# Attention start of a fused attention and mixture-of-experts kernel: another order for the first two heads

## The chip, the cores and the metric

The kernel runs on one core of a Trainium2 chip. The metric is the device time of one execution in microseconds (us), as the median of several runs. The five engines are TensorE (PE, with its weight loads as PEld), VectorE (DVE), ScalarE (ACT), GpSimd (POOL) and SyncE (SP). SP only issues DMAs; ACT and POOL can issue DMAs too. Each engine takes its own instructions strictly in the order in which they were recorded.

## The reference, cut to what matters

Sixteen heads (2 batches of 8) of attention over 768 positions with 64 dimensions, masked by a hash: six signs of a projection give each query and each key a bucket, and only equal buckets see each other.

```
q_bits = (np.einsum('bhsd,dk->bhsk', q, proj) > 0)      # the same for k
mask = q_bucket[:, :, :, None] == k_bucket[:, :, None, :]
scores = np.where(mask, scale * np.matmul(q, k.transpose(0, 1, 3, 2)), -1e9)
scores = scores - np.max(scores, axis=-1, keepdims=True)
attn = np.exp(scores); attn = attn / (np.sum(attn, axis=-1, keepdims=True) + 1e-09)
return np.matmul(attn, v)
```

The result goes through a mixture of experts (8 experts, one per token, 1536 tokens of 512) and a gated two-layer network (512 to 2048 and back).

## The kernel before, in words

The program is one long list, written in the order in which it is to run: no scheduler moves anything. The attention comes first and ends near 230 us; the experts follow until about 397 us, then the two-layer network.

The attention works head by head. A head has four tiles, X, Y, K1 and K2 (one of four sets, taken in turn), which hold q and k, scaled and split into a high and a low part (hi and lo, made on ACT and by a subtraction), and rows that carry the hash signs (the bits). `prep0` fills the tiles of heads 0 to 2, `prep` those of the later heads, where SP's DMAs place hi, lo and bits (`put_bits`). `bits` makes the signs: products with the projection on PE into the tiles psb, then two sign operations on DVE into tile b.

Before a head's scores are taken, each row's maximum must be known. `mx` (line 454 on) multiplies X and K2 into tiles psm, two products of 384 columns for each sixth of the head, and DVE takes the maxima (line 457); there are three psm buffers. After the sixth part, DVE forms `top` (line 460), and SP sends it into row 76 of X (line 461). `scores(k)` (lines 466 to 474) is step k of 96, six steps to a head: four products (pst, from Y and K1 and from X and K2), and two exponentials on ACT into a tile pf. `high` rounds pf to 16 bits (phi, on ACT or DVE), `low` takes the rest (plo, a subtraction on POOL), and `pv` multiplies both with the values (psv). There are four pf buffers, so an exponential also waits for plo of four steps before, and two pst buffers.

The values are scaled by a power of two. `vmax` takes maxima of the values on DVE, `vscale` turns them into one scale for four heads: a transposition on PE (psn), a maximum on DVE, a product (pso), and some ten small DVE operations, the result being sc. `vsplit(h)` writes the scaled values of a head in 16 bits on ACT and their rest by a SCALAR_TENSOR_TENSOR on DVE (lines 717 to 719); `vgate` makes the gate's columns of the same tile (vh), by products psg, a copy gv, transpositions and four small DVE operations. `heat` issues PE products on a tile of zeros that nothing reads.

The steps from `run(pre[0])` to `first = ...` (lines 756 to 789) are written out by hand. After that a loop over k issues in turn `scores(k)`, the roundings, `mx` of later parts as the table entry `ac` says, and `pv`; `at`, `spread` and `stages` place all other work at fractions of k, from the numbers in the table Q.

Of the kernel before, what the change touches and what calls it, by code (L numbers as in the profile page):

```python
# [13 lines left out]
AF = mybir.ActivationFunctionType  # L14
ALU = mybir.AluOpType
# [5 lines left out]
B, H, S, D = 2, 8, 768, 64  # L21
# [42 lines left out]
def moe_attention_kernel(ctx, tc, qk, v, vt, pj, wg, w1, w2, win, wout, out, cap):  # L64
# [8 lines left out]
    def f32(t):  # L73
        return t.bitcast(F32)

    def run(gen):
        for _ in gen:
            pass
# [229 lines left out]
                )  # L308


    Q = {'v': (-3.25, -4.75, -1.75, -2.25), 'vg': (-6.5, -6.75), 'vgd': 1, 'pr': (-13.0, -12.75, -12.0, -12.5), 'prd': 0.6, 'b0': 7.75, 'b': 1.75, 'bd': 0.5, 'vm0': (9.0, 9.25, 10.75, 13.0), 'vm': (-0.5, 4.75, 7.0, 12.25), 'vs': 13.25, 'pa': 1.5, 'ev': 0.5, 'lvt': -5.0, 'v4': (2.0, 4.25, 8.0, 16.25), 'vg0': (1.85, -4.4, 8.0), 'p2': 3.5, 'lr': (0.25, 1.25, 5.5), 'lv': 6.25, 'vsd': 0.75, 'ac': (0, 0, 2, 4, 6, 7, 8, 10), 'hd': (3, 5, 17), 'hn': (1, 3, 2, 0, 2, 0, 0, 0), 'ap': (0,), 'h0': (7,), 'hl': (6,), 'l0': (), 'll': (1, 3), 'ht': (6, 3, 7, 6, 3, 2)}


    HT = Q["ht"]
# [1 line left out]
    with ExitStack() as actx:  # L316
# [13 lines left out]
        def heat(pool_, tag, n, cols=512):  # L330

            if pool_ not in heat_t:
                heat_t[pool_] = pool_.tile([P, 512], F32, tag=tag, name=f"heat{tag}")
            for _ in range(n):
                pe.matmul(heat_t[pool_][:, :cols], idle_sb[:, 0:P], idle_sb[:, :cols], start=True, stop=True)  # L335
# [22 lines left out]
        def load_r(h):  # L358
            rt[h] = pr.tile([P, S], F32, tag="r", name=f"r{h}")
            sp.dma_start(out=rt[h], in_=qk[h])  # L360
# [47 lines left out]

        def put_bits(h):
            st = sets[h % 4]  # L410
            b = b_t[h // 4]
            o = 32 * (h % 4)
            sp.dma_start(out=f32(st["X"])[D : D + 12], in_=f32(b)[o : o + 12])
            sp.dma_start(out=f32(st["K2"])[D : D + 12], in_=f32(b)[o + 12 : o + 24])

        def signs(out, ps, c):
            dve.tensor_scalar(out=out, in0=ps, scalar1=0.0, scalar2=c, op0=ALU.is_gt, op1=ALU.subtract)
# [45 lines left out]
        def scores(k):  # L463
            h, j = divmod(k, NC)
            st = sets[h % 4]
            pf = pf_t[k] = pt.tile([P, S], F32, tag="pf", name=f"pf{k}", bufs=4)
            kc = slice(j * P, (j + 1) * P)
            for n in range(2):
                ps = ps_t.tile([P, 512], F32, tag="t", name=f"pst{k}{n}")
                qc = slice(n * HS, (n + 1) * HS)  # L470
                pe.matmul(ps[:, :HS], st["K1"][:, kc], st["Y"][:, qc], start=True, stop=False)  # L471
                pe.matmul(ps[:, :HS], st["K2"][0:77, kc], st["X"][0:77, qc], start=False, stop=True)  # L472
                act.activation(  # L473
                    pf.rearrange("k (c n p) -> k c n p", c=NC, n=2)[:, :, n],
                    ps[:, :HS].rearrange("k (p c) -> k c p", c=NC), AF.Exp, scale=0.125 / SC / SC,
                )
# [234 lines left out]
        def vsplit(h):  # L711
            g = h // 4
            r = vr_t[g][:, h % 4]
            s = sc_t[g][:, 0:1]
            t = vh(h)
            o = E * (1 - h % 2)
            act.activation(t[:, :, o : o + D], r, AF.Copy, scale=s)
            yield
            dve.scalar_tensor_tensor(
                out=t[:, :, VA + o : VA + o + D], in0=r, scalar=s, in1=t[:, :, o : o + D],  # L720
                op0=ALU.mult, op1=ALU.subtract,
            )
            dve.memset(t[:, :, DE:VA], 1.0)
            if h > 3:
                c = t[:, :, VA + o : VA + o + 1]
                pool.tensor_copy(c, c)
# [37 lines left out]
        b0 = bits(0, [ps_v.tile([P, 512], F32, tag="v", name=f"psb0{n}") for n in range(2)])  # L764
        for n in range(NC):
            mx(n)
        run(pre[1])
        load_r(4)
        next(b0)
        for i in range(4):  # L770
            vmax(0, i)
        vs = vscale(0)
        next(vs)
        next(vs)
        next(b0)
        heat(ps_t, "t", 2)
        next(vs)
        next(vs)
        next(b0)
        put_bits(1)  # L780
        scores(0)
        run(b0)
        run(vs)
        next(pre[2])
        put_bits(2)
        run(pre[2])
        first = vsplit(0), vgate(0)
        next(first[1])
        next(first[1])
# [20 lines left out]
        def at(k, f, *args):  # L810
            later.setdefault(k, []).append((f, args))

        def spread(k, gen, d=1):


            def part(k):
                if next(gen, gen) is not gen:
                    n = k + (d if k < STEPS - NC * 2 else min(d, 1) * 0.75)
                    at(n, part, n)

            at(k, part, k)

        def stages(gen, ks):
            for k in ks:
                at(k, next, gen, None)

        stages(first[1], (1, 1.5, 2, 2.75, 3.25))
        spread(1, first[0], 0.75)
        for i in range(3):
            at(Q["lr"][i], load_r, 5 + i)  # L830
        for g in range(1, G):
# [7 lines left out]
            at(max(0, 24 * (h // 4 - 1) - 2) + h % 4 / 4, load_r, h)  # L839
        for h in range(3, NH):  # L840
            if h == 3:
                spread(2.25, prep(h), 3)
            else:
                spread(NC * h + Q["pr"][h % 4], prep(h), Q["prd"])
        for h in range(1, NH):
# [711 lines left out]
```

## Time and profile before

| | |
|---|---|
| Median of 3 runs | 661.85 us (661.36 to 662.96) |
| Profiled execution | 664.08 us |
| Its span | 662.3 us |
| PE busy | 630.1 us (95%) |
| PEld busy | 469.5 us (71%) |
| DVE busy | 472.1 us (71%) |
| ACT busy | 435.1 us (66%) |
| POOL busy | 232.2 us (35%) |
| Chain that ended last | PE 55%, ACT 3%, DMA 3%, DVE 2% |

Busy shares are means over stages with different limits. The change lies in the first 60 us, so only rows of that stretch tell what it moves, and rows of the later stages tell whether a shift of the start reaches the end. PE's busy time counts a product from its start to its modelled end, and products overlap, so the distance from one start to the next tells more than the length.

### The profile page before, as it was taken

What the parts mean: (1) busy time and instruction counts of PE and PEld (TensorE: products, weight loads), DVE (VectorE), ACT (ScalarE), POOL (GpSimd) and SP (SyncE); (2) the same over time, 40 slices, a digit from 0 to 9 for tenths busy, and PEclk for the clock granted to TensorE, in tenths of its full rate; (3) what the DMA queues carried; (4) which work ended last, traced back from release to release, by engine and by line L of the source; (5) the groups of instructions that cost most, each with busy time, mean ns of one, the idle gap of its engine ahead of it and who ended that gap; (6) DMA issues with size and microseconds to landing.
All of it is one profiled execution on the core that took longest, in us unless ns stands there. A gap on an engine that the chain in (4) does not pass through costs nothing.

```text
span 662.3 us, 14355 instructions
## 1 busy us (share of the span) xinstructions
PE 630.1 (95%) x5497; PEld 469.5 (71%) x5497; DVE 472.1 (71%) x1042; ACT 435.1 (66%) x880; POOL 232.2 (35%) x217
## 2 busy tenths in 40 slices
PE   6999999999999799999999999999999999999892
PEld 2678889889888669999999995555555555555440
DVE  6788988888879888888888888888888342222410
ACT  8658868878878746777776755455545585555820
POOL 6457879879896052111566300000000030000021
PEclk9999999999999989999999999999999999999997
DMA  5645864774465158777677643443441020000011
GB/s 195 175 125 136 243 168 125 237 184 126 103 176 187 57 174 309 242 249 236 214 248 253 212 138 107 141 154 131 127 147 46 0 80 17 0 1 1 0 50 52
DMA packets 37843, 92.18 MB, mean 139 GB/s; under 512 B 8986, under 2 KB 14362, under 8 KB 37762
## 3 DMA queue, kind: packets, MB, share of 16 engines
q1 hardware_dynamic: 34674, 83.75, 41.9%
q0 software_dynamic: 2400, 7.36, 3.2%
q8 instruction: 46, 0.75, 0.5%
q14 instruction: 35, 0.29, 0.1%
q10 hardware_dynamic: 688, 0.03, 0.1%
HBM read 67.14 MB, written 6.29 MB: 111 GB/s over the span
## 4 chain that ended last, share of the span: by engine, by line
PE 55%; ACT 3%; DMA 3%; DVE 2%; issue 1%; POOL 0%; POOLq 0%
PE psg L1332 17%; PE pso L1359 15%; PE psy L1110 11%; PE psh L1083 10%; DMA out_dram<-os,inv 3%; ACT junk L1286 2%; PE psa L1060 1%; ACT gh L1342 1%; DVE rl L1335 1%; DVE wl L164 1%; PE heat L1162 0%; ACT rl L1334 0%; ACT wh L158 0%; ACT hh L1086 0%; PE heatt L335 0%
## 5 line engine op out<-in xcount | busy, mean ns | idle before, releaser
L487 POOL TENSOR_TENSOR plo<-pf,phi 128x768 f16<-128x768 f32 x86 | 144.9, 1706 | 32.8 <-ACT phi L481 16.7
L457 DVE TENSOR_REDUCE mx<-psm 128x1 f32<-128x384 f32 x192 | 96.8, 550 | 20.6 <-PE psm L454 19.9
L473 ACT ACTIVATE pf<-pst 128x384 f32<-128x384 f32 x192 | 83.4, 486 | 40.3 <-PE pst L472 35.8
L1374 POOL DMA_INDIRECT out_dram<-os,inv x12 | 12.1, 1012 | 272.6 <-DVE os L1366 244.3
L164 DVE SCALAR_TENSOR_TENSOR wl<-raw,wh 128x1024 f16<-128x1024 f32 (+1 forms) x68 | 82.5, 1216 | 6.2 <-ACT wh L158 5.4
L1332 PE MATMUL psg<-yTh,ch 128*128 128x512 f16 (+1 forms) x256 | 83.4, 326 | 3.2 <-DVE rl L1335 3.2
L1332 PE MATMUL psg<-yTl,ch 128*128 128x512 f16 (+1 forms) x256 | 83.4, 326 | 0.0
L1332 PE MATMUL psg<-yTh,cl 128*128 128x512 f16 (+1 forms) x256 | 83.4, 326 | 0.0
L1335 DVE SCALAR_TENSOR_TENSOR rl<-rl,psg 128x512 f32<-128x512 f32 x64 | 35.0, 551 | 64.4 <-ACT rl L1334 64.0
L471 PE MATMUL pst<-Y,K 128*128 128x384 f32 x192 | 75.7, 394 | 2.3 <-ACT pf L473 2.3
L1332 PEld LDWEIGHTS <-ch 128*128 128x128 f16 x512 | 50.1, 98 | 35.9
L481 ACT ACTIVATE phi<-pf 128x768 f16<-128x768 f32 x85 | 71.7, 844 | 1.9
L1359 PE MATMUL pso<-ch,gh 128*128 128x512 f16 x192 | 72.8, 379 | 0.0
L1359 PE MATMUL pso<-ch,gl 128*128 128x512 f16 x192 | 72.8, 379 | 0.0
L1359 PE MATMUL pso<-cl,gh 128*128 128x512 f16 x192 | 72.8, 379 | 0.0
L158 ACT ACTIVATE wh<-raw 128x1024 f16<-128x1024 f32 (+1 forms) x68 | 67.4, 998 | 0.8 <-DVE offs L959 0.8
L1359 PEld LDWEIGHTS <-gh 128*128 128x128 f16 x384 | 37.6, 98 | 42.3
L454 PE MATMUL psm<-K,X 76*128 76x384 f32 x192 | 64.3, 419 | 2.8 <-DVE mx L457 1.1
L472 PE MATMUL pst<-X,K 77*128 77x384 f32 x192 | 66.3, 346 | 0.5 <-DMA X<-top 0.5
L1110 PE MATMUL psy<-hh,wl 128*128 128x224 f16 x256 | 66.3, 259 | 0.2 <-DVE wl L164 0.2
L1110 PE MATMUL psy<-hh,wh 128*128 128x224 f16 x256 | 66.3, 259 | 0.0
L1110 PE MATMUL psy<-hl,wh 128*128 128x224 f16 x256 | 66.3, 259 | 0.0
(243 smaller groups left out, 1485.6 us busy)
## 6 DMA issues: line engine op xcount, KB each, us to landing
raw<-in_w_dram SPq DMA_DIRECT2D x64, 512.0 KB
rc<-in_win_dram SPq DMA_DIRECT2D x16, 512.0 KB
rc<-in_wout_dram SPq DMA_DIRECT2D x16, 512.0 KB
r<-in_qk_dram SPq DMA_DIRECT2D x16, 384.0 KB
K<-hi SPq DMA_DIRECT2D x26, 192.0 KB
vr<-in_v_dram SPq DMA_DIRECT2D x4, 768.0 KB
vt<-in_vt_dram SPq DMA_DIRECT2D x8, 384.0 KB
K<-lo SPq DMA_DIRECT2D x16, 192.0 KB
```

Source lines behind the costliest of these rows:

```text
L158: act.activation(wh[e, i][:, c : c + n], r, AF.Copy, scale=(S1, S2)[i // 2])
L164: dve.scalar_tensor_tensor(out=wl[e, i][:, c : c + n], in0=r, scalar=(S1, S2)[i // 2], in1=wh[e, i][:, c : c + n], op0=ALU.mult, op1=ALU.s ...
L457: dve.tensor_reduce(out=mm[:, c, n : n + 1], in_=ps[:, :HS], axis=AX.X, op=ALU.max)
L471: pe.matmul(ps[:, :HS], st["K1"][:, kc], st["Y"][:, qc], start=True, stop=False)
L472: pe.matmul(ps[:, :HS], st["K2"][0:77, kc], st["X"][0:77, qc], start=False, stop=True)
L473: act.activation(pf.rearrange("k (c n p) -> k c n p", c=NC, n=2)[:, :, n], ps[:, :HS].rearrange("k (p c) -> k c p", c=NC), AF.Exp, scale=0 ...
L481: act.activation(phi_t[k], pf_t[k], AF.Copy)
L487: eng.tensor_tensor(out=plo_t[k], in0=pf_t.pop(k), in1=phi_t[k], op=ALU.subtract)
L1083: pe.matmul(ps, l[:, c], r[:, k], start=n == 0, stop=n == 3 * KD - 1)
L1110: pe.matmul(ps, l, r, start=n == 0, stop=n == 3 * KF - 1)
L1332: pe.matmul(ps, l, x, start=n == 0, stop=n == 3 * KD - 1)
L1359: pe.matmul(po[blk][s], l, r, start=first and n == 0, stop=last and n == 2)
```

## The change

Six edits, all at the start of the attention:

- in the maxima of head 0, an idle product of 512 columns follows each of the six parts;
- the scores of step 0 are issued before the products of the scale, and both sign operations of the first bits before the scale's second maximum;
- `put_bits` of heads 1 and 2 follows at once, before lo of head 1 is sent; X's rows go by SP, K2's by POOL's queue;
- the rests of the values of heads 0 and 1 are taken by POOL, for which ACT writes the scaled values a second time, in place, in 32 bits;
- lo of head 2 (`pre[2]`) moves from before the steps to 5.5, `prep` of head 3 from 2.25 and 5.25 to 7 and 8.25;
- the first maxima of head 1 are issued at step 1 instead of step 2.

```diff
-    'ac': (0, 0, 2, 4, 6, 7, 8, 10)
+    'ac': (0, 1, 3, 4, 6, 7, 8, 10)
...
         def put_bits(h):
             st = sets[h % 4]
+            q = pool if h < 3 else sp
...
-            sp.dma_start(out=f32(st["K2"])[D : D + 12], in_=f32(b)[o + 12 : o + 24])
+            q.dma_start(out=f32(st["K2"])[D : D + 12], in_=f32(b)[o + 12 : o + 24])
...
             act.activation(t[:, :, o : o + D], r, AF.Copy, scale=s)
-            yield
-            dve.scalar_tensor_tensor(
-                out=t[:, :, VA + o : VA + o + D], in0=r, scalar=s, in1=t[:, :, o : o + D],
-                op0=ALU.mult, op1=ALU.subtract,
-            )
+            if h in (0, 1):
+                act.activation(r, r, AF.Copy, scale=s)
+            yield
+            lo = t[:, :, VA + o : VA + o + D]
+            if h in (0, 1):
+                pool.tensor_tensor(out=lo, in0=r, in1=t[:, :, o : o + D], op=ALU.subtract)
+            else:
+                dve.scalar_tensor_tensor(
+                    out=lo, in0=r, scalar=s, in1=t[:, :, o : o + D], op0=ALU.mult, op1=ALU.subtract
+                )
...
         for n in range(NC):
             mx(n)
-        run(pre[1])
-        load_r(4)
+            heat(ps_x, "x", 1)
         next(b0)
         for i in range(4):
             vmax(0, i)
         vs = vscale(0)
         next(vs)
+        scores(0)
+        next(b0)
+        next(b0)
+        put_bits(1)
         next(vs)
-        next(b0)
-        heat(ps_t, "t", 2)
+        heat(ps_v, "v", 1)
         next(vs)
         next(vs)
-        next(b0)
-        put_bits(1)
-        scores(0)
-        run(b0)
+        put_bits(2)
         run(vs)
-        next(pre[2])
-        put_bits(2)
-        run(pre[2])
+        run(pre[1])
+        load_r(4)
...
+        at(5.5, run, pre[2])
...
             if h == 3:
-                spread(2.25, prep(h), 3)
+                stages(prep(h), (7, 8.25))
```

On PE the prediction speaks of the place after the bits' products (psb): psn and pso are the products of the scale, pst the scores (pst00 and pst01 of step 0, pst10 of step 1), the tiles heat are idle. Before:

```order
L428 MATMUL psb01_248<-r3_175,pj_sb_137 32x384
L610 MATMUL psn0_307<-ident_64,am10_304 2x128
L335 LDWEIGHTS idle_sb_135
L335 MATMUL heatt_310<-idle_sb_135 128x512
L619 MATMUL pso0_317<-dg_315,ones_65 128x2
L471 MATMUL pst00_323<-Y0_139,K10_140 128x384
L472 MATMUL pst00_323<-X0_138,K20_141 128x384
L471 MATMUL pst01_327<-Y0_139,K10_140 128x384
L472 MATMUL pst01_327<-X0_138,K20_141 128x384
```

Now, up to the first maxima of head 1 (psm100, psm101):

```order
L429 MATMUL psb01_248<-r3_175,pj_sb_137 32x384
L472 MATMUL pst00_311<-Y0_139,K10_140 128x384
L473 MATMUL pst00_311<-X0_138,K20_141 128x384
L472 MATMUL pst01_315<-Y0_139,K10_140 128x384
L473 MATMUL pst01_315<-X0_138,K20_141 128x384
L611 MATMUL psn0_323<-ident_64,am10_307 2x128
L620 MATMUL pso0_331<-dg_329,ones_65 128x2
L472 MATMUL pst10_361<-Y0_139,K10_140 128x384
L455 MATMUL psm100_372<-K21_145,X1_142 128x384
L455 MATMUL psm101_375<-K21_145,X1_142 128x384
L564 MATMUL psg0_378<-vt0_180,wg_sb_74 32x256 x3
L472 MATMUL pst20_392<-Y0_139,K10_140 128x384
```

Step 0's scores stand ahead of psn and pso, and head 1's first maxima stand ahead of the gate's products and of step 2; idle products between these rows are left out.

On DVE, the maxima of head 1 (psm100 is part 0, first half), where lo2 is the low part of head 2 and vh0 the values of head 0. Before:

```order
L639 COPY isw_75<-sc0_334 128x1
L372 SCALAR_TENSOR_TENSOR lo2_242<-r2_173,hi2_240 128x768
L568 COPY gv0_377<-psg0_369 96x256
L457 TENSOR_REDUCE mx1_159<-psm100_394 128x1
L457 TENSOR_REDUCE mx1_159<-psm101_397 128x1
L457 TENSOR_REDUCE mx1_159<-psm110_401 128x1
L457 TENSOR_REDUCE mx1_159<-psm111_404 128x1
L719 SCALAR_TENSOR_TENSOR vh0_373<-vr0_177,sc0_334,vh0_373 128x6x64
L723 MEMSET vh0_373 128x6
L457 TENSOR_REDUCE mx1_159<-psm120_432 128x1
```

Now:

```order
L640 COPY isw_75<-sc0_338 128x1
L458 TENSOR_REDUCE mx1_159<-psm100_372 128x1
L458 TENSOR_REDUCE mx1_159<-psm101_375 128x1
L569 COPY gv0_387<-psg0_378 96x256
L458 TENSOR_REDUCE mx1_159<-psm110_404 128x1
L458 TENSOR_REDUCE mx1_159<-psm111_407 128x1
L458 TENSOR_REDUCE mx1_159<-psm120_411 128x1
L458 TENSOR_REDUCE mx1_159<-psm121_414 128x1
L729 MEMSET vh0_382 128x6
```

The two SCALAR_TENSOR_TENSOR rows are gone from between the maxima (lo2 stands behind those of head 1 now), and the copy gv0 stands among them.

On POOL, between lo of head 1 and the first rests. Before:

```order
L760 DMA xd_62<-fill_163 16x1x32
L390 TENSOR_TENSOR lo1_232<-rs1_233,hi1_230 128x768
L487 TENSOR_TENSOR plo0_392<-pf0_322,phi0_355 128x768
L487 TENSOR_TENSOR plo1_430<-pf1_357,phi1_379 128x768
L487 TENSOR_TENSOR plo2_466<-pf2_381,phi2_419 128x768
```

Now:

```order
L766 DMA xd_62<-fill_163 16x1x32
L390 TENSOR_TENSOR lo1_232<-rs1_233,hi1_230 128x768
L415 DMA K21_145<-b0_294 12x768
L415 DMA K22_149<-b0_294 12x768
L488 TENSOR_TENSOR plo0_402<-pf0_310,phi0_358 128x768
L724 TENSOR_TENSOR vh0_382<-vr0_177,vh0_382 128x6x64
L488 TENSOR_TENSOR plo1_433<-pf1_360,phi1_389 128x768
```

Two DMAs that wait for the bits, and a subtraction of the values (a second one follows behind plo3), stand in front of the rests.

## Rows read from the trace of the kernel before

**Rows 1.** Windows: busy us (instructions) of PE, PEld, DVE, ACT, POOL; granted clock, DMA, GB/s.
```profile
130.00:145.00 15.00, 15.00 (x204) 12.37 (x202) 13.27 (x27) 11.35 (x22) 11.30 (x10) 1.00 0.73 185
```

**Rows 2.** Timeline 8 to 20 us: start, length, engine, line, operation, [idle before <- releaser].
```profile
8.52 5.67 DVE L457 TENSOR_REDUCE mx<-psm 128x1 f32<-128x384 f32 x12 [0.32 <-PE psm L454]
...
14.42 0.52 SPq L461 DMA_DIRECT2D X<-top  x1
...
16.55 0.61 DVE L417 TENSOR_SCALAR b<-psb,pj_sb 128x384 fp32r<-128x384 f32 x1
...
18.45 0.69 PE L471 MATMUL pst<-Y,K 128*128 128x384 f32 x1
...
19.26 0.52 PE L471 MATMUL pst<-Y,K 128*128 128x384 f32 x1
...
19.47 0.17 DVE L633 TENSOR_SCALAR sc<-ex 128x3 int32<-128x3 int32 x1
19.55 1.07 ACT L473 ACTIVATE pf<-pst 128x384 f32<-128x384 f32 x2 [2.59 <-PE pst L472]
19.58 0.52 PE L472 MATMUL pst<-X,K 77*128 77x384 f32 x1
```

**Rows 3.** Timeline of ACT, 21 to 41 us.
```profile
21.41 0.95 ACT L473 ACTIVATE pf<-pst 128x384 f32<-128x384 f32 x2
...
22.25 0.61 ACT L717 ACTIVATE vh<-vr,sc 128x384 f16<-128x384 f32 x1
22.76 0.83 ACT L481 ACTIVATE phi<-pf 128x768 f16<-128x768 f32 x1
...
24.48 0.85 ACT L368 ACTIVATE hi<-r 128x768 fp32r<-128x768 f32 x1
...
30.18 0.87 ACT L473 ACTIVATE pf<-pst 128x384 f32<-128x384 f32 x2 [1.75 <-POOL plo L487]
...
40.87 0.87 ACT L473 ACTIVATE pf<-pst 128x384 f32<-128x384 f32 x2 [2.46 <-PE pst L472]
```

**Rows 4.** Timeline of DVE, 20 to 37 us.
```profile
20.06 0.95 DVE L372 SCALAR_TENSOR_TENSOR lo<-r,hi 128x768 fp32r<-128x768 f32 x1
...
23.18 0.42 DVE L568 COPY gv<-psg 96x256 f32<-96x256 f32 x1 [2.18 <-PE psg L563]
...
24.71 1.95 DVE L457 TENSOR_REDUCE mx<-psm 128x1 f32<-128x384 f32 x4 [1.10 <-PE psm L454]
...
26.58 1.62 DVE L719 SCALAR_TENSOR_TENSOR vh<-vr,sc,vh 128x384 f16<-128x384 f32 x1
...
35.06 2.01 DVE L719 SCALAR_TENSOR_TENSOR vh<-vr,sc,vh 128x384 f16<-128x384 f32 x1
```

**Rows 5.** Timeline of SP and PE, 33 to 36 us: head 1's maxima sent, and its first scores.
```profile
33.29 0.51 SPq L461 DMA_DIRECT2D X<-top  x1
...
35.39 0.41 PE L472 MATMUL pst<-X,K 77*128 77x384 f32 x1 [0.46 <-DMA X<-top]
...
35.64 0.34 PE L471 MATMUL pst<-Y,K 128*128 128x384 f32 x1
...
35.82 0.34 PE L472 MATMUL pst<-X,K 77*128 77x384 f32 x1
```

**Rows 6.** The tile K up to 40 us: its DMAs by POOL's queue, issue to landing.
```profile
L758 POOL DMA_DIRECT2D K<-fill x4: 494/514/702, 8.3 to 10.0; - x4
...
DMA to landing us min/median/max: 3.0/3.2/3.5
```

**Rows 7.** Timeline of POOL: the second rest.
```profile
23.67 1.65 POOL L487 TENSOR_TENSOR plo<-pf,phi 128x768 f16<-128x768 f32 x1 [0.45 <-ACT phi L481]
```

**Rows 8.** Timelines of DVE and PE, 41 to 47 us.
```profile
41.39 1.02 DVE L457 TENSOR_REDUCE mx<-psm 128x1 f32<-128x384 f32 x2 [1.51 <-PE psm L454]
...
46.85 0.63 PE L563 MATMUL psg<-vt,wg_sb 128*32 128x256 f32 x6 [1.11 <-DVE b L417]
```

**Rows 9.** Windows at the end of the attention, columns as in rows 1.
```profile
226.00:230.00 4.00, 2.01 (x22) 1.05 (x22) 3.28 (x14) 3.25 (x11) 0.00 (x0) 1.00 0.13 31
230.00:232.00 2.00, 1.07 (x10) 0.55 (x11) 0.63 (x5) 0.00 (x0) 0.00 (x0) 0.52 0.26 57
```

More of the change, by code (lines that the diff above doesn't have):

```diff
@@ L308, in windows @@
                 )
-    Q = {'v': (-3.25, -4.75, -1.75, -2.25), 'vg': (-6.5, -6.75), 'vgd': 1, 'pr': (-13.0, -12.75, -12.0, -12.5), 'prd': 0.6, 'b0': 7.75, 'b': 1.75, 'bd': 0.5, 'vm0': (9.0, 9.25, 10.75, 13.0), 'vm': (-0.5, 4.75, 7.0, 12.25), 'vs': 13.25, 'pa': 1.5, 'ev': 0.5, 'lvt': -5.0, 'v4': (2.0, 4.25, 8.0, 16.25), 'vg0': (1.85, -4.4, 8.0), 'p2': 3.5, 'lr': (0.25, 1.25, 5.5), 'lv': 6.25, 'vsd': 0.75, 'ac': (0, 0, 2, 4, 6, 7, 8, 10), 'hd': (3, 5, 17), 'hn': (1, 3, 2, 0, 2, 0, 0, 0), 'ap': (0,), 'h0': (7,), 'hl': (6,), 'l0': (), 'll': (1, 3), 'ht': (6, 3, 7, 6, 3, 2)}
+    Q = {'v': (-3.25, -4.75, -1.75, -2.25), 'vg': (-6.5, -6.75), 'vgd': 1, 'pr': (-13.0, -12.75, -12.0, -12.5), 'prd': 0.6, 'b0': 7.75, 'b': 1.75, 'bd': 0.5, 'vm0': (9.0, 9.25, 10.75, 13.0), 'vm': (-0.5, 4.75, 7.0, 12.25), 'vs': 13.25, 'pa': 1.5, 'ev': 0.5, 'lvt': -5.0, 'v4': (2.0, 4.25, 8.0, 16.25), 'vg0': (1.85, -4.4, 8.0), 'p2': 3.5, 'lr': (0.25, 1.25, 5.5), 'lv': 6.25, 'vsd': 0.75, 'ac': (0, 1, 3, 4, 6, 7, 8, 10), 'hd': (3, 5, 17), 'hn': (1, 3, 2, 0, 2, 0, 0, 0), 'ap': (0,), 'h0': (7,), 'hl': (6,), 'l0': (), 'll': (1, 3), 'ht': (6, 3, 7, 6, 3, 2)}
     HT = Q["ht"]
```

## The prediction

> **What bounds the kernel now.** I read the windows first, then the timeline of the first 50 us engine by engine, then what each engine waits for. In the long middle of the attention PE is busy in every microsecond of the window, with the other engines between 75% and 90% [rows 1]; in this in-order pipeline what counts is when it is filled. If head 1 and head 2 reach PE some microseconds earlier, everything behind them in the lists moves with them, as nothing later is tied to a fixed time: all later loads are issued in the order of the same lists. So I look for the lead that the change gives at the end of the start-up, near 47 us, and carry it to the end.
>
> The start is not bound by PE. DVE first takes twelve maxima without a pause [rows 2], sends them, and step 0's scores come only at 18.45, its exponential at 19.55 [rows 2]. From 24.71 to 33.26 DVE is without a gap again: head 1's maxima, with a value split of 1.62 us between them [rows 4]; when they are sent (33.29), PE waits for them to land, until 35.39 [rows 5]. That is 2.10 us from issue to use. Near 35 us the next split takes 2.01 us [rows 4], and the maxima of head 2 queue behind it. From 41.39 DVE is busy without a gap until PE, which has waited 1.11 us for its signs, goes on at 46.85 [rows 8]. So DVE's list, three times, sets the start.
>
> **The change part by part.** The profiled execution took 664.08 us with a span of 662.3, so 1.8 lie around the span; it stands 2.2 above the median of 661.85. The sum is a difference in its trace, and I take it off the median.
>
> *Idle products in head 0's maxima.* DVE needs 5.67 / 12 = 0.47 us for each maximum [rows 2], so 0.94 for a pair. PE's products of 384 columns start 0.32 apart at 19 us (19.26 to 19.58) [rows 2] and 0.18 apart at 35 us (35.64 to 35.82) [rows 5], the spacing of 1.2 and 2.4 GHz, though the profile gives the granted clock as full for both. By that a 512-column product costs 0.43 or 0.24 (an estimate, by columns). A pair with its idle product is 2 x 0.32 + 0.43 = 1.07 at the low clock, 0.13 over DVE's pace, or 0.60 at the high one. Six pairs cost between 0 and 0.8. I take 0.35, as if the clock rose midway, since PE now has no pause there. Head 0's maxima are then sent at 14.8 and land at 16.9.
>
> *Scores ahead of the scale.* PE's list puts step 0's four products right behind the bits, so they start when the maxima land, 16.9. The exponential begins at about 17.3 instead of 19.55: 2.25 earlier. The price: psn, the scale's transposition, stands behind them, and its maximum stands behind both sign operations (0.6 each, from about 17.05 now, 16.55 before [rows 2]). So signs end at 18.25 and the scale comes at about 20.4 instead of 19.5 (the row of sc) [rows 2]. Step 1's scores wait behind pso: its exponential comes at 19.9 instead of 21.41 [rows 3]. The lead has shrunk to 1.5.
>
> *Bits by two queues.* K2's bits go by POOL's queue at 18.3. Nearest rows: POOL's own DMAs into K landed after 3.0 to 3.5 us [rows 6]; SP's maxima were usable after 2.10 [rows 5]. I take 3.2, the same queue and tile: landed at 21.5. The bounds are 2.1 and 3.5; the end of the idle products ahead of them (20.8) caps the gain. PE's list now has head 1's first maxima ahead of the gate's products and of step 2, so those wait with them. POOL's rests stand behind these DMAs, but the first rest waits for phi (about 19.05) anyway: nothing.
>
> *Splits by POOL, lo2 later.* From its first maximum to the send DVE took 24.71 to 33.26, 8.55 us. Without the split (-1.62) and with the copy gv, which stood ahead of it (+0.42) [rows 4], it needs 7.35; lo2 (0.95) is behind now, and its senders K1 and Y are not read before step 12. First product 21.5, first maximum 0.5 later at 22.0, send at 29.35; I add 0.3 for parts that PE brings late. Sent at 29.7, usable at 31.8: **3.6 ahead** of 35.39 [rows 5]. ACT must keep up: from 19.9 on it owes for steps 1 to 5 five exponentials (0.9) and five roundings (0.83), two splits and two new copies of 0.61 each [rows 3], 11.1 us in all, thus 31.0 without waits, 31.7 with the waits for step 4. It fits, just. The hi of head 3 (0.85), which stood at 24.48 [rows 3], is gone from here; it stands behind step 7's exponential now. Step 4's exponential comes at 27.0 against 30.18. POOL's two subtractions are half as wide as the rest of 1.65 [rows 7], so 0.85 each (bounds: 0.6, the width at DVE's price without its wait, and 1.65); POOL waits for phi between rests, and an exponential needs the rest of four steps before: step 5's, at 29.9, needs one that ends near 24.6. So they cost nothing.
>
> *Head 2's maxima.* Before, the split of 2.01 held them until 37.07, and step 8's exponential came at 40.87, 3.8 later [rows 3, 4]. Now that split is POOL's work and lo2 fits while DVE waits for the scores of step 6. The maxima start at 33.0, the exponential comes at 36.8: **4.1 ahead**.
>
> *Head 3's low part.* It stood near 34 us; it now stands between two maxima and the first signs of the next bits, in the very list that is without a gap from 41.39 to 46.85 [rows 8]. It costs its 0.95 in full (the length of lo2 [rows 4]; with POOL busy up to 1.2). 46.85 - 4.1 + 0.95 = 43.7: **3.1 ahead**.
>
> Moved past on SP: the maxima of head 1 no longer wait behind hi of head 3, and the load r7 stands behind lo2's sends now, near 33.0 instead of 36.8; PE needs it at about 37.4, before 41.5. That is 4.4 us instead of 4.7, no wait or 0.3. The tiles of head 3 land near 42, needed near 45.
>
> Sum: 3.1 us of lead, kept by a PE that has no slack behind [rows 1]. 661.85 - 3.1 = **658.8 us**. Bounds: K2's bits at 20.8 (0.7 more) and lo3 hidden (0.95 more) give 657.1; the cases below give the other end.
>
> **A rule against the queue.** K's DMAs on POOL took 3.0 to 3.5 us while DVE worked beside them, not the 2.10 of SP [rows 5, 6]. The Trainium skill, SBUF — State Buffer, section "SBUF: two separate sides", says that DMAs of GpSimd's queue have their descriptors written by GpSimd, which certain DVE operations lock out for as long as they last. By that rule the bits would land late by the length of such operations; those that stand at that time are the scale's, 0.17 us like the row of sc [rows 2], so the sum would stay; it is what would feed the third rival.
>
> **The rivals.**
> *The clock falls again.* At 226 to 230 PE was busy for 2.01 of 4 us, and behind that the granted clock was 0.52, the 1.2 GHz level [rows 9]. Between psb and 21.5 the new order leaves PE busy for some 3.3 of 5.7 us, hardly more. The Trainium skill, TensorE: Matmul & The Clock Gate, Part 1, has the clock fall to half after idling and rise with sustained work; the rows agree for the end of the attention. If it falls, head 1's first six products, the gate's and steps 2 and 3 run at 0.32 instead of 0.18 until it rises; ten such products and some idle ones cost 1.4 to 2, of which 1.4 arrives at step 3's exponential: a lead of 1.7, **660.2 us**. Against it: the spacing was 0.18 by 35 us in the old order, which had pauses too [rows 5].
> *The lead is used up behind the start.* If r7, head 3's tiles or DVE's signs are later than I worked out, heads 2 and 3 return to the old times. Up to 2.8 of 3.1 goes: **661.5 us**. For it: several transfers lose their cushion at once. Against it: they need 3 us each, and the cushions are 0 to 3.
> *The bits on POOL's queue land late.* Each microsecond beyond 21.5 holds PE, which has head 1's first maxima ahead of step 2, and moves DVE's run of 7.35 one for one. With 6.3 us from issue to landing the gain is zero; at 8.5 us the kernel is slower, **664.1 us**. Against it: no DMA of this queue took over 3.5 us here [rows 6]; for it: these have 12 partitions, those one.
> *The scale is the bound.* It comes 0.9 later than before; if value splits, not maxima, held the first values' products, step 0's gain would be nothing. They are not needed before step 5's turn, so this is only a part of the second case.
>
> **How the numbers follow.** The forecast, a lead of 2.1 to 4.0, gets 0.60; more than that 0.05; the clock 0.15; the lead used up 0.11; late bits 0.09. A measurement of this kernel can tell about 0.3% from no change, which is 2.0 us, so faster means below 659.9. Forecast and more: 0.65 faster. Clock and used up: 0.26 the same. Late bits: 0.09 slower. The range takes in the bounds 657.1, less 0.3 for the spread of medians, up to the second rival: 656.8 to 661.5. Left out is 0.09 of late bits and some 0.06 on either side.
>
> **What would show it.** In the profile after: step 0's exponential near 17.3, step 1's near 19.9, no SCALAR_TENSOR_TENSOR between head 1's maxima, their send near 29.7 and first use near 31.8, step 8 near 36.8, the gate's products of the next heads near 43.7, and the end of the attention 3 us earlier. Wrong if head 1's first product comes after 23 us, if products of 384 columns are 0.32 apart at 22 us, or if the lead at 47 us is not there at 100.

## The result, and the profile after

| | before | after |
|---|---|---|
| Median of 7 runs each, in turn | 661.85 us (659.99 to 663.79) | 666.43 us (664.15 to 668.32) |
| Ratio to before, 95% interval | | 1.0064 (1.0039 to 1.0090) |
| Span of the profiled execution | 662.3 us | 666.6 us |
| Step 8's exponential | 40.87 us | 39.26 us |
| Step 10's exponential | 48.14 us | 51.25 us |
| Step 28's exponential | 87.75 us | 92.73 us |
| Last product of the two-layer network | 649.49 us | 654.39 us |

The kernel became slower by 0.64%, outside the predicted range. (Here and below a ratio is formed from runs side by side, so it differs a little from the quotient of the two medians.) Steps are counted from 0; the exponential that the expectations below call step 24's, at 87.75 before, is step 28's by this count and has that name here. The exponentials of the steps show where the time went: at step 8 the changed kernel still led by 1.6 us, at step 10 it lagged by 3.1, at step 12 by 4.8 (56.88 against 52.06). From there on the lag stays between 4.6 and 5.4 (5.2 at the first product behind the attention, psh, 247.30 against 242.09; 4.9 at the last product of the two-layer network).

The timeline of the changed kernel, all engines, in order of time (start, length, engine, line, operation, idle time before and what ended it). Line numbers are those of the changed kernel, one to seven above those of before.

```profile
8.75 0.65 PE L335 MATMUL heatx<-idle_sb 128*128 128x512 f16 x1
9.76 5.39 DVE L458 TENSOR_REDUCE mx<-psm 128x1 f32<-128x384 f32 x10 [0.21 <-PE psm L455]
9.84 0.65 PE L335 MATMUL heatx<-idle_sb 128*128 128x512 f16 x1
...
15.38 0.52 SPq L462 DMA_DIRECT2D X<-top  x1
...
18.19 0.34 PE L472 MATMUL pst<-Y,K 128*128 128x384 f32 x1
18.36 0.33 PE L473 MATMUL pst<-X,K 77*128 77x384 f32 x1
...
18.45 0.87 ACT L474 ACTIVATE pf<-pst 128x384 f32<-128x384 f32 x2 [1.49 <-PE pst L473]
18.93 1.05 POOL L415 DMA_DIRECT2D K<-b  x2 [3.65 <-DVE b L418]
20.27 1.64 POOL L488 TENSOR_TENSOR plo<-pf,phi 128x768 f16<-128x768 f32 x1 [0.29 <-ACT phi L482]
20.30 1.63 DVE L629 TENSOR_SCALAR am<-am 128x2 int32<-128x2 int32 x1
...
21.93 0.75 PE L455 MATMUL psm<-K,X 76*128 76x384 f32 x2 [0.37 <-DMA X<-b]
22.28 0.17 DVE L634 TENSOR_SCALAR sc<-ex 128x3 int32<-128x3 int32 x1
...
31.91 0.52 SPq L462 DMA_DIRECT2D X<-top  x1
...
36.57 0.43 SPq L590 DMA_DIRECT2D vr<-in_v_dram  x1
37.77 0.47 SPq L400 DMA_DIRECT2D X<-hi  x1
...
39.26 0.87 ACT L474 ACTIVATE pf<-pst 128x384 f32<-128x384 f32 x2 [1.51 <-PE pst L473]
...
42.83 4.84 POOL L488 TENSOR_TENSOR plo<-pf,phi 128x768 f16<-128x768 f32 x3 [4.80 <-PE psv L502]
...
45.64 0.55 DVE L594 TENSOR_REDUCE am<-vr 128x1 f32<-128x384 f32 x1 [1.83 <-DMA vr<-in_v_dram]
46.10 1.98 DVE L726 SCALAR_TENSOR_TENSOR vh<-vr,sc,vh 128x384 f16<-128x384 f32 x1
...
48.48 0.60 DVE L418 TENSOR_SCALAR b<-psb,pj_sb 128x384 fp32r<-128x384 f32 x1
...
49.14 1.07 PE L564 MATMUL psg<-vt,wg_sb 128*32 128x256 f32 x6 [5.00 <-DVE b L418]
...
51.25 1.07 ACT L474 ACTIVATE pf<-pst 128x384 f32<-128x384 f32 x2 [8.10 <-PE pst L473]
```

The same place in the timeline of the kernel before, rows that were not shown yet:

```profile
37.90 0.44 SPq L589 DMA_DIRECT2D vr<-in_v_dram  x1
...
43.74 5.17 POOL L487 TENSOR_TENSOR plo<-pf,phi 128x768 f16<-128x768 f32 x3 [4.31 <-PE psm L454]
...
44.68 0.54 DVE L593 TENSOR_REDUCE am<-vr 128x1 f32<-128x384 f32 x1
45.14 0.66 DVE L719 SCALAR_TENSOR_TENSOR vh<-vr,sc,vh 128x384 f16<-128x384 f32 x1
...
48.14 0.87 ACT L473 ACTIVATE pf<-pst 128x384 f32<-128x384 f32 x2 [3.38 <-PE pst L472]
```

Windows of the changed kernel, columns as in [rows 1]:

```profile
38.00:40.00 2.00, 2.00 (x32) 1.82 (x32) 0.49 (x2) 0.74 (x2) 0.03 (x1) 1.00 1.06 351
...
44.00:46.00 2.00, 0.14 (x4) 0.00 (x0) 0.36 (x1) 0.00 (x0) 2.00 (x2) 1.00 1.07 228
46.00:48.00 2.00, 0.00 (x0) 0.00 (x0) 2.00 (x2) 0.00 (x0) 1.67 (x2) 1.00 0.97 186
48.00:50.00 2.00, 0.86 (x6) 0.19 (x6) 1.93 (x7) 0.00 (x0) 0.00 (x0) 0.68 0.23 63
50.00:52.00 2.00, 2.00 (x9) 1.86 (x7) 0.08 (x1) 0.66 (x2) 0.00 (x0) 0.50 0.00 0
...
56.00:58.00 2.00, 2.00 (x17) 1.83 (x14) 0.60 (x2) 1.09 (x3) 1.49 (x1) 1.00 0.89 230
```

What to see there, in this order. Values of heads 4 to 7 (vr, 768 KB) are loaded by one DMA. It is issued at 36.57, 1.33 earlier than before, yet DVE waits for it until 45.64, where before the same maximum ran at 44.68 without a wait. The difference is what follows on SP's queue: before, nothing (head 3's hi went out at 25 to 28 us); now, from 37.77, head 3's four hi transfers, its bits and its lo, some 1 MB in all, and the DMA engines are full up to 48 us. From its issue to the end of its last packet the load takes 8.3 us, before 6.2. On DVE the signs of the next bits stand behind that maximum, one more and a split. The split itself takes 1.98 instead of 0.66. POOL's rests run beside it in both kernels (the rows at 42.83 and 43.74); what differs is where it meets them. In the kernel before it began 0.25 us ahead of the end of a rest (45.39) and ended 0.41 behind that end. Now, held back by the load, it begins 0.07 behind the start of a rest (46.03 to 47.67), and again ends 0.41 behind its end. PE's gate products (psg) wait for these signs, 5.00 us instead of the 1.11 of [rows 8]. PE is then idle from 44 to 49, and the granted clock falls to 0.50, the 1.2 GHz level; it is back at 1.00 only at 56 us.

The lag is thus made of two parts of like size: psg starts 2.29 later than before (49.14 against 46.85; 0.96 of it is the later maximum and 1.32 the longer split), and another 2.5 is added up to step 12, where products run at the low clock (4.82 at step 12).

### The profile page after: what moved, and what is told of

Same layout as the page of the kernel before. It is cut to its first block, busy times and chain, and to the rows that moved or that the text cites. A ratio compares the mean times of both kernels' runs of the same rounds, so it can differ in the third digit from the quotient of the medians.

```text
span 666.6 us, 14367 instructions
## 1 busy us (share of the span) xinstructions
PE 629.6 (94%) x5500; PEld 470.3 (71%) x5500; DVE 473.2 (71%) x1040; ACT 436.2 (65%) x882; POOL 235.0 (35%) x221
## 4 chain that ended last, share of the span: by engine, by line
PE 56%; ACT 3%; DMA 2%; DVE 1%; issue 1%; POOL 0%; POOLq 0%
PE psg L1337 16%; PE pso L1364 15%; PE psy L1115 11%; PE psh L1088 11%; DMA out_dram<-os,inv 2%; ACT junk L1291 1%; PE psa L1065 1%; ACT gh L1347 1%; DVE rl L1340 1%; PE heat L1167 0%; ACT rl L1339 0%; DVE wl L164 0%; PE heatt L335 0%; POOL out_dram L1379 0%; DVE os L1371 0%
```

## The experiments

Two theories came out of the traces. **T**: vr's landing shares the transfers with head 3's moved sends and holds the chain from DVE's maxima to PE. **U**: DVE's own list (lo of head 3, the split) holds the signs, and the transfer is a side matter. **V** concerns the front: idle products and a late scale cost more than was taken. All edits are made to the changed kernel (those with 'lv', 'vm0', 'l0' and 'vg0' change one entry of the table Q); the medians of the kernel before, run beside them, lay between 661.07 and 661.79 us.

### The load first

```diff
-    ... 'lv': 6.25 ...
+    ... 'lv': 2.9 ...
```

> One edit to the changed kernel: the load of the next four heads' values (vr1) is issued at step 2.9 instead of 6.25, so ahead of head 1's maxima, not right before head 3's hi. Theory T (the moved sends of head 3's hi share the transfer engines with vr1, which lands at 45.5 and holds DVE's maxima and behind them the bits' second signs, on which PE's gate products wait): DVE no longer waits 1.8 us for vr1, PE's gate products come at 46 to 47.3 instead of 49.14, PE's pause is under 3 us instead of 5.0, and the time is 661 to 664. Theory U (DVE's own list, with head 3's low part of 0.95 and a split of 1.98 in it, holds the signs): the gate products stay after 48 and the time stays at 665 to 667. Theory V (the idle products and the later scale are what costs): no change, 666.

Measured: 661.39 us, ratio 1.0001 (0.9975 to 1.0028). Timeline of this kernel:

```profile
23.14 0.43 SPq L590 DMA_DIRECT2D vr<-in_v_dram  x1
...
43.68 0.55 DVE L594 TENSOR_REDUCE am<-vr 128x1 f32<-128x384 f32 x1
...
45.91 0.63 PE L564 MATMUL psg<-vt,wg_sb 128*32 128x256 f32 x6 [1.69 <-DVE b L418]
...
47.19 0.87 ACT L474 ACTIVATE pf<-pst 128x384 f32<-128x384 f32 x2 [3.96 <-PE pst L473]
```

T holds: one number of the table takes the ratio from 1.0064 back to 1.0001, 4 to 5 us. The first part up to step 8 is unchanged (39.22); psg comes 3.23 earlier than in the changed kernel, and its windows from 44 to 54 us show a clock of 1.00. The load takes 6.3 us from issue to its last packet, as before the change. The split takes 0.72 here, so this edit removes its stall beside POOL along with the wait; the experiment with the splits by DVE, below, has the wait without the stall. What is left is a lead of 0.95 over the kernel before at psg and at step 10, 1.8 at step 28, too little for the medians to tell.

### Head 2's and head 3's preparations moved back

```diff
-        at(5.5, run, pre[2])
+        at(0.75, run, pre[2])
...
-                stages(prep(h), (7, 8.25))
+                spread(2.25, prep(h), 3)
```

> One part of the change undone: the low part of head 2 stands at step 0.75 and the preparation of head 3 at 2.25 and 5.25, near where they stood before; the other five edits stay. T: head 3's sends are done before vr1 is issued, vr1 lands before its maxima, gate products at 44 to 46, no fall of the clock near 50, time 658 to 661. U: the same, as head 3's low part leaves the list too. V: the gate products move little, time 665 to 667.

Measured: 662.53 us, ratio 0.9999 (0.9972 to 1.0027), above the expected 658 to 661; psg comes at 47.35, later than the expected 44 to 46. Timeline:

```profile
16.82 0.87 ACT L474 ACTIVATE pf<-pst 128x384 f32<-128x384 f32 x2
...
26.45 0.55 PE L455 MATMUL psm<-K,X 76*128 76x384 f32 x1 [2.25 <-DVE mx L458]
...
41.39 0.87 ACT L474 ACTIVATE pf<-pst 128x384 f32<-128x384 f32 x2 [2.24 <-PE pst L473]
...
47.35 0.63 PE L564 MATMUL psg<-vt,wg_sb 128*32 128x256 f32 x6 [1.08 <-DVE b L418]
```

The loss is gone here too, as T has it, but U expected the same, so this run does not tell the two apart. The gain is gone as well: from step 0 to step 8 it takes 24.57 us (41.39 - 16.82), against 20.81 in the changed kernel. With lo2 and head 3's work ahead, lo2 takes 2.29 us on DVE beside a rest of POOL (0.95 in [rows 4]), PE waits 2.25 us for DVE's maxima (the row at 26.45) and the clock falls to 0.50 behind that:

```profile
28.00:30.00 2.00, 2.00 (x7) 1.33 (x7) 1.30 (x4) 1.64 (x3) 1.16 (x2) 0.50 0.98 276
```

So without the moves of lo2 and of head 3 the lead is gone at step 8, and the same moves put head 3's sends behind vr. How much of the 3.8 us is either move and how much the clock, this run does not tell.

### The signs ahead of the two maxima

```diff
-    ... 'vm0': (9.0, 9.25, 10.75, 13.0) ...
+    ... 'vm0': (9.5, 9.75, 10.75, 13.0) ...
```

> One edit to the changed kernel: the first two maxima of vr1's values stand at 9.5 and 9.75, behind the bits' second signs instead of ahead of them; loads and sends as they are. T: vr1 still lands near 45, but nothing that PE waits for stands behind it; gate products at 46 to 47, time 661 to 664. U: the split of 1.98 still stands ahead of the signs, so the gate products come at 48 or later, time 664 to 667. V: no change, 666.

Measured: 665.54 us, ratio 1.0041 (1.0016 to 1.0065), a miss. Timeline:

```profile
19.33 0.52 PE L473 MATMUL pst<-X,K 77*128 77x384 f32 x1
19.65 0.52 PE L472 MATMUL pst<-Y,K 128*128 128x384 f32 x1
...
45.95 0.63 PE L564 MATMUL psg<-vt,wg_sb 128*32 128x256 f32 x6 [1.35 <-DVE b L418]
...
46.67 0.55 DVE L594 TENSOR_REDUCE am<-vr 128x1 f32<-128x384 f32 x1 [0.78 <-DMA vr<-in_v_dram]
...
50.93 0.99 PE L455 MATMUL psm<-K,X 76*128 76x384 f32 x2 [3.45 <-DMA K<-b]
```

The gate products come 3.2 earlier, as expected. Then PE stops again for 3.45 us, now at head 3's first maxima, whose bits land late in the same crowd (by the row, PE waits for them), and the clock falls to 0.50 during that wait. The chain over DVE is only one arm of the fault; the crowd of transfers also holds head 3's own tiles. That is why moving the load mends it and moving the signs doesn't. Besides, the clock fell at step 1 in this execution (products 0.32 apart), so that step 8 came 22.74 us after step 0 instead of 20.81; psg still came early.

### No idle products

```diff
-            heat(ps_x, "x", 1)
```

> One part of the change undone: no idle products among head 0's maxima; all else as changed. All theories: head 0's maxima are sent at 14.4 as before the change, 1.0 earlier than now. T: that microsecond is lost again at vr1 or reaches the end at most in full, time 665 to 667. V: step 8 comes 1 us earlier and the end 3 us or more, time under 663.5. If the idle products are what keeps the clock up, step 0's products start 0.32 us apart instead of 0.18 and step 0's exponential gains less than 0.6.

Measured: 664.40 us, ratio 1.0030 (1.0006 to 1.0054). Step 0's exponential comes at 17.17, step 8's at 38.18, and 1.1 of lead over the changed kernel at step 8 grows to 3.2 at the first product behind the attention (psh 244.06 against 247.30). PE still waits 3.40 at psg, and the clock falls. The time lies between what T (665 to 667) and V (under 663.5) expected, and the interval overlaps that of the changed kernel. So V holds in part, as far as the idle products go and against the one profile of the changed kernel; the last experiment shows that this is not their price in every execution.

### The load first and no idle products

Both edits above together.

> The changed kernel without the idle products in the maxima and with the next group's value load (vr1) sent at 2.9 instead of 6.25: two of the causes found are taken away together. If they add up (theory T for the load, V for the idle products): head 0's last maximum is sent at 14.4, the first exponential starts near 17.2, step 8's near 38.2 (39.2 with the load first alone), the maximum of vr1 waits for no transfer, the gate product psg comes near 45.0 with no fall of the clock behind it, step 24's exponential near 85.0 (85.97 with the load first alone), and the time is 659.0 to 660.5. Rival N: the lead is lost again between steps 8 and 24 because something else there (DVE's own list before the signs) ends last; then step 8 is at 38.2 but step 24 stays at 86.0 or later and the time is 661 to 662, as with the load first alone.

Measured: 661.66 us, ratio 0.9989 (0.9973 to 1.0004). Windows:

```profile
46.00:48.00 2.00, 2.00 (x7) 2.00 (x7) 0.28 (x1) 1.06 (x3) 0.82 (x1) 0.50 0.00 0
```

They do not add up; time and exponential are those of rival N. Step 8 is where it was expected (38.09), psg too (44.78), but PE waited 1.81 us there for the signs from DVE, it was busy for 0.97 and 1.22 of 2 us in the two windows from 42 to 46, the clock fell to 0.50 behind that, and step 28 came at 87.02, later than with the load first alone. That DVE's list ends last there is N's own reason; the fall of the clock behind it was in neither: it took back what the front had given.

### The first rest by DVE

```diff
-    ... 'l0': () ...
+    ... 'l0': (0,) ...
```

> The changed kernel with one edit: the first rest of the exponentials (plo0) is made by DVE behind the scale instead of by GpSimd beside it. Theory P: the scale's second small operation on DVE (128x2, line 629) took 1.63 us because GpSimd's subtraction of 1.64 us ran at the same time; without it the operation takes 0.17 to 0.2 us, the scale sc is there at 20.8 instead of 22.3, and step 2's exponential starts 0.6 to 1.4 earlier than 24.39. Rival: the operation waits for something that isn't shown (a semaphore, the access of PSUM); then it stays at 1.5 us or more and sc at 22.3. Neither theory takes away vr1's late landing, so step 24's exponential stays within 1 us of 92.7 and the time is 665 to 667.5.

Measured: 667.21 us, ratio 1.0071 (1.0043 to 1.0099). Timeline:

```profile
20.00 0.17 DVE L629 TENSOR_SCALAR am<-am 128x2 int32<-128x2 int32 x1
...
20.51 0.17 DVE L634 TENSOR_SCALAR sc<-ex 128x3 int32<-128x3 int32 x1
```

P holds for the operation: 0.17 us instead of 1.63 when POOL doesn't subtract beside it. It is worth little. In this execution step 0 was 0.48 earlier than in the changed kernel already, step 2 is 0.75 earlier and step 8 0.52, so that the whole stall of 1.46 on DVE buys 0.3 at step 2 and nothing at step 8.

### All three together

The load first, no idle products, the first rest by DVE.

> All three together: vr1 sent at 2.9, no idle products, plo0 on DVE behind the scale. Theory P with T and V: sc near 19.8, step 2's exponential near 22.3, step 8's near 37.5, step 24's near 84.5, and the time 658.0 to 660.0, 0 to 1 below the kernel with the first two alone. Rival: DVE is the one that is late after 22, so that 0.9 us more on it costs what the scale gains: step 8 no earlier than 38.2 and the time the same as with the first two alone or above.

Measured: 661.54 us, ratio 0.9996 (0.9975 to 1.0017). Step 8 comes at 37.79, 0.3 earlier than without the third edit; the clock falls as with the first two (0.50 from 46 to 52 us), and step 28 is at 86.91. The time is the rival's, that of the first two edits alone, though step 8 is nearer to P's 37.5. The third edit changes nothing in the time that can be measured.

### Splits by DVE, and bits by SP

Two kernels, each with one edit. The first has the split of heads 0 and 1 on DVE again, without ACT's second copy; the second sends all bits by SP:

```diff
-            q = pool if h < 3 else sp
+            q = sp
```

> The changed kernel with one edit: the splits of the values of heads 0 and 1 are made by DVE again (no second copy on ACT, no subtraction on GpSimd). If the splits by GpSimd are worth what the prediction took (DVE free of 1.6 to 2.0 us each, ACT held for 0.6 each), step 8's exponential comes 0.3 to 1.5 later than 39.26 and the time is 666 to 668. Rival: the split by GpSimd costs as much as it saves, since its subtraction of 0.89 holds DVE's operations beside it and the copies hold the exponentials: step 8 at 39.3 or earlier. In both vr1's landing still ends last before the gate products (psg 48.5 to 49.5, waiting over 3 us), so the time stays above 664.

Measured: 667.63 us, ratio 1.0084 (1.0054 to 1.0114). From step 0 to step 8 it takes 39.60 - 17.96 = 21.64 us, against 20.81: the splits by POOL are worth 0.8. The gates' products wait 2.62 only, since PE reaches them 1.3 later and the split of head 2 takes 0.65 here; they come at 48.07, and the loss stays (57.04 at step 12, 5.0 behind the kernel before):

```profile
46.36 0.65 DVE L724 SCALAR_TENSOR_TENSOR vh<-vr,sc,vh 128x384 f16<-128x384 f32 x1
```

So the loss is there without the stall of the split.

> The changed kernel with one edit: the K2 bits of heads 1 and 2 are sent by SP again, as before the change. If GpSimd's queue is worth what the prediction took (SP free 0.8 us earlier for each, landings alike), head 1's products of the maxima come 0 to 0.8 later than 21.93, step 8's exponential 0 to 0.8 later than 39.26, and the time is 666 to 667.5. Rival: GpSimd's sends landed late and their loss was hidden; then step 8 comes earlier by over 0.3 and the time is below 666. vr1's landing is not touched, so the loss of 4 to 5 us between steps 9 and 12 stays in both.

Measured: 664.96 us, ratio 1.0041 (1.0021 to 1.0061), below the expected 666. By its letter the rival came true (step 8 earlier by 0.39, under 666), but in this execution step 0 was 0.61 earlier already. From step 0 to step 8 it takes 38.87 - 17.84 = 21.03, so POOL's queue is worth 0.2; the loss behind step 9 stays (step 10 at 50.85, step 28 at 93.71). The median is 1.5 below the changed kernel's, with intervals that overlap, and the trace gives no ground for it; whether this is more than the spread stays open.

### All that helps, and signs first

The load first, no idle products, and the two maxima behind the signs ('vm0' 9.5, 9.75).

> The kernel with the load first (2.9) and without idle products, and in it DVE's two first maxima of vr1 put behind the second signs of group 1 ('vm0' 9.5, 9.75 instead of 9.0, 9.25). There step 8's exponential led by 2.8 and step 10's by 1.3 only: PE waited at psg (44.78, 1.81) for the second signs, which stood behind two maxima (0.54 each) and a split (0.72) on DVE. Theory G (that wait spends the lead): the signs come 1.0 earlier, psg at 43.4 to 43.9, step 10's exponential at 45.2 to 46.2, no clock fall, step 24's at 85.0 to 86.0 and the time 658.5 to 660.5. Rival H: head 3's maxima products (psm) behind them wait for head 3's tiles (bits and rests by SP) instead, so that step 10 gains 1 and step 12 (51.28) nothing; then step 24 stays at 86.5 to 87.5 and the time at 661 to 662.

Measured: 659.70 us, ratio 0.9963 (0.9946 to 0.9980), the fastest version here. Timeline:

```profile
43.90 0.60 DVE L418 TENSOR_SCALAR b<-psb,pj_sb 128x384 fp32r<-128x384 f32 x1
...
44.56 0.63 PE L564 MATMUL psg<-vt,wg_sb 128*32 128x256 f32 x6 [1.36 <-DVE b L418]
...
45.84 0.87 ACT L474 ACTIVATE pf<-pst 128x384 f32<-128x384 f32 x2 [3.62 <-PE pst L473]
```

G holds, though psg comes 0.7 later than it had it. The edit that failed alone works where the load no longer crowds head 3's tiles: no second wait, the clock at 1.00 from 40 to 58 us, and the lead over the kernel before, 2.3 at step 10, is 2.7 at step 28 and 3.6 at the last product of the two-layer network.

### Gate products two steps later

The load first, no idle products, and

```diff
-    ... 'vg0': (1.85, -4.4, 8.0) ...
+    ... 'vg0': (1.85, -4.4, 10.0) ...
```

> The same kernel (load first, no idle products) with the gate products of heads 2 and 3 put two steps later (8.0 to 10.0), so that PE passes on to step 10's and 11's scores without a wait for the second signs. Theory G: step 10's exponential near 44 (46.82 before this edit), no clock fall at 44 to 50, psg later than 47 but not waited for; step 24's exponential at 84.5 to 86.0, the time 658 to 660.5. Rival H: the products of head 3's maxima or the evaluation of the gates, now 2 to 3 us later, are waited for at steps 12 to 14 (psv of head 2 needs them), and step 24 stays at 86.5 or later, the time at 661 or above.

Measured: 661.69 us, ratio 1.0005 (0.9990 to 1.0020). Timeline:

```profile
43.98 0.87 ACT L474 ACTIVATE pf<-pst 128x384 f32<-128x384 f32 x2 [1.64 <-PE pst L473]
...
56.60 0.27 PE L611 MATMUL psn<-ident,am 128*1 128x128 f32 x1 [1.94 <-DVE vh L581]
```

Step 10 comes at 43.98, 4.2 ahead of the kernel before, but at step 28 (86.02) 1.7 are left, and the time is rival H's. PE waits 1.43 at head 3's first maxima, by the profile for a send into X, and then 1.94 for the gates' evaluation on DVE, which is later now. The wait that was stepped over comes back later.

### Load and signs first, with the idle products

> The changed kernel with the load first (2.9) and the second signs ahead of the two maxima (9.5, 9.75), but with its idle products: beside the same kernel without them (659.7, step 8 at 38.33, step 24 at 85.06) this gives their price where no clock fall comes between. Theory I (they cost what they hold head 0's maxima, about 1 us, carried to the end): step 0's exponential at 18.4, step 8's at 39.3, step 10's at 46.8, step 24's at 85.5 to 86.5, the time 660 to 661.3. Rival K (they pay, by keeping the clock up where it falls without them): step 0's at 18.4 all the same, but step 24's at 85.0 or earlier and the time at or below 659.7.

Measured: 660.65 us, ratio 0.9983 (0.9969 to 0.9998), within theory I's time, though its profiled execution shows neither picture: step 0 at 16.93, step 8 at 37.81, step 28 at 85.16. Timeline of its first maxima:

```profile
8.57 0.39 PE L335 MATMUL heatx<-idle_sb 128*128 128x512 f16 x1
9.30 0.39 PE L335 MATMUL heatx<-idle_sb 128*128 128x512 f16 x1
...
14.20 0.52 SPq L462 DMA_DIRECT2D X<-top  x1
```

Here idle products follow each other 0.73 and then (four times) 0.93 apart, the pace of DVE's maxima, against 1.09 in the changed kernel's profile: by this spacing the clock had risen before 8.57. The maxima are sent at 14.20. The profiles of all kernels that have idle products fall into these two kinds and no third: three (the moves back, the signs first, this one) sent at 14.08 to 14.27, the other five, the changed kernel among them, at 15.20 to 15.38. Without idle products the send comes at 14.21 to 14.39, and step 0's exponential at 17.09 to 17.27; with them it comes at 16.82 to 16.98 in the first kind and at 17.84 to 18.45 in the second. So idle products give some 0.3 us in the one and cost 0.6 to 1.4 in the other. In three of the five kernels without them the windows show a granted clock of 0.85 to 0.88 from 8 to 12 us and 0.50 from 12 to 16: it had been up there and fell during head 0's maxima. Against the same kernel without idle products (659.70, on another chip) the median is 0.95 higher, which agrees with a cost in part of the executions; the two intervals overlap, and what decides the kind of an execution stays open.

## Why the prediction was wrong

**The step that failed** is the paragraph "Moved past on SP". It took the load r7, the maxima of head 1 and head 3's tiles, and left out vr, the largest transfer of that stretch, which is issued behind r7 and vt and now has head 3's sends right behind it. The paragraph goes through SP's queue transfer by transfer, and this one was missing: 384 KB of r7, 384 of vt, 768 of vr, 768 of hi, 72 of bits and 192 of lo are 2,568 KB between 35.5 and 45.6 us, 260 GB/s, which is what the windows show for full DMA engines (186 to 351). Sharing with these, the load's last packet ends at 44.91 and DVE takes its maximum at 45.64, while the prediction had psg, which waits for signs behind that load, at 43.7: "Head 3's low part" carried a lead of 4.1 through DVE's list as if nothing in it waited for a transfer. In its place there was a wait of 1.83 us on DVE, a split of 1.98, and psg 2.29 later than before. The first experiment shows that the load's place is the cause, the third that the crowd works through head 3's tiles as well.

**The way from 3.1 ahead to 4.8 behind** has three pieces of like size: 2.5 are missing at step 8 (a lead of 1.6 instead of 4.1), 2.9 more go between there and psg beyond the 0.95 that was reckoned, and 2.5 to the low clock up to step 12.

**"Kept by a PE that has no slack behind"** was right for the sign that was not expected: the lag of 4.8 us at step 12 is 4.9 at the last product of the two-layer network, 654 us.

**The clock.** The first rival placed a fall near 21 us. In the profiled execution it did not fall there: products start 0.17 apart at 18.36, better than the 0.32 of [rows 2]. It fell between 48 and 50, after PE's idle time, and added 2.5 us, about half of the lag against the kernel before. The mechanism of [rows 9] was right, its place was not. (In the third experiment's execution it did fall at step 1; the 1.9 us that this cost by step 8 are what the rival had taken, 1.4 to 2.) The Trainium skill, TensorE: Matmul & The Clock Gate, Part 1, has the clock halve after idle time; the trace agrees, with 0.14 and 0.00 busy of 2 us ahead of a granted clock of 0.50.

**Mis-sized terms, all before step 9.** The idle products were taken as 0.35, half of 0 to 0.8: they were 0.96 here (sent at 15.38 against 14.42 [rows 2]) and nothing in other executions, never a half. Step 0's exponential came at 18.45 instead of 17.3, and 1.1 ahead of before instead of 2.25. The scale came at 22.28 instead of 20.4, mostly because DVE's small operation took 1.63 us beside POOL's rest; yet the sixth experiment shows that this cost only 0.3 at step 2. Head 1's maxima were sent at 31.91 instead of 29.7: DVE started 0.9 later (22.87 instead of 22.0) and then waited 1.5 for PE's parts where I had added 0.3. At step 8 the lead was 1.6 instead of 4.1.

**Right terms.** K2's bits: POOL's two DMAs landed after 2.6 to 2.7 us, and head 1's first product came at 21.93, predicted 21.5; the third rival, late bits, did not occur: those DMAs waited for the signs (the row at 18.93), and the trace shows no other wait. The subtractions of the splits took POOL 0.89 each, reckoned 0.85. That the splits by POOL gain is right in direction; they gave 0.8 up to step 8, where 1.62 had been taken off for head 1 alone. The moves of lo2 and head 3 are right in direction too: without them step 0 to step 8 takes 3.8 longer, in an execution in which the clock also fell on the way. All parts together gained little there, since from step 0 to step 8 it takes 20.81 us against 21.32 before; the prediction had 19.5.

**The second rival**, "the lead is used up", named the right kind of cause, transfers that lose their cushion. Its bound was wrong: it let heads 2 and 3 fall back to the old times at worst, as if a crowd of transfers could only spend a lead. Nothing bounds it there.

## What to carry to other kernels

When a group of sends is moved, write down every transfer that is in flight between its new place and its first reader, with bytes, and divide by the rate that the trace shows for full DMA engines; a large load ahead of the group is slowed too (here from 6.2 to 8.3 us). A late transfer costs twice if PE idles for it, once as a wait and again as a low clock behind it. And an earlier front is only worth what the next in-order waits let through: the same edit (signs first) failed where transfers were crowded and paid where they were not.

## What the runs showed of the hardware

A DVE operation on 128x2 integers, 0.17 us long, took 1.63 us beside a subtraction of POOL of 1.64: it began 0.03 after POOL's and ended at 21.93, POOL's at 21.91. In the sixth experiment, with POOL idle, it took 0.17 again. The Trainium skill, SBUF — State Buffer, section "SBUF: two separate sides", describes a port pair which DVE and GpSimd share, and which one instruction holds to its end against certain kinds of DVE operation; the two ends agree with that.

The split of the values on DVE took 0.61 us wherever no rest of POOL stood beside its start. In the traces of all fourteen kernels 111 splits began with more than 0.2 us of a rest of POOL left; each ended 0.41 or 0.42 us behind the end of that rest, which made the same operation 0.63 to 2.01 us long. So a wait that only moves the start of a split can cost up to 1.4 us more.

With idle products and the same order up to step 0, PE's clock, by the spacing of products, had risen ahead of 8.6 us in the profiles of three kernels and not before the maxima were over in those of five others. Step 0's exponential came at 16.82 to 16.98 in the ones and at 17.84 to 18.45 in the others.
